# One explicit order for the first 2256 steps of a fused attention and MLP kernel

## The chip, the core and the metric

The kernel runs on one core of a Trainium2 chip. The core has a matrix engine (TensorE, called PE in the profile, with its weight loads as PEld), a vector engine (DVE), a scalar engine (ACT), GpSimd (POOL) and a queue that issues transfers (SP). Each engine works through its own list of instructions in the order in which the program issued them, and they wait for one another by semaphores. The metric is device time in microseconds (us) of the whole program; the median of three runs of the kernel before is 1229.67 us (1228.19 to 1231.2).

## The reference

Attention over 8 batches, 12 heads, 448 positions and 64 dimensions, with a root-mean-square norm on q and k, and then an MLP with ELU on the 3584 tokens of 768 features:

```python
q_n, k_n = rmsnorm(q, g_q), rmsnorm(k, g_k)
scores = matmul(q_n, k_n.transpose(0, 1, 3, 2)) / sqrt(64)
attn = softmax(scores)                       # minus the row's maximum, sum + 1e-9
x = matmul(attn, v).transpose(0, 2, 1, 3).reshape(3584, 768)
h = x @ w_in                                 # 768 x 2048
g = where(h > 0, h, exp(min(h, 0)) - 1)
out = g @ w_out                              # 2048 x 768
```

## The kernel before

Heads go in pairs: 48 pairs, six to a batch, and a pair has seven score tiles of 128 x 448, so there are 336 tiles T. Large products are made of float16 parts: a value is split into a high and a low half, and a product is three matmuls (high x high, high x low, low x high).

The steps, by the names that the text uses (lines are those of the profile):

- Per pair p: load q and k (L345), square them on ACT (`qk_square`, L368), sum (DVE, L372), root by logarithm and exponential on ACT (L376, L377), norm on POOL (L397), copies to float16 on ACT (L406, L416), low halves on POOL, transposes by transfer (L435), swapped halves (L442).
- Per tile T: the score matmuls (`s_mm`, L578), the row maximum on DVE (`s_max`, L585), the exponential on ACT (`s_exp`, L601), reciprocal (L613). The 42 tiles of batch 0 then make a scaled diagonal on POOL (`s_diag`, L617), are transposed by PE (`s_pe`, L625) and copied out by ACT (`s_hi`, L635). Later tiles are scaled by ACT (`s_hi`, L645), get a low half from DVE (`s_lo`, L651) and are transposed by transfers (`s_tr`, L661).
- Per pair: `attend` (L678) multiplies with v into the bank `av`; ACT and DVE write the result as x(p) in two halves (`x_high` L685, `x_low` L692 or L697).
- Weights: the 16 blocks of w_in and the 24 blocks of w_out are turned into high and low halves once, in the kernel's first part, each by nine steps (`conv`): a load (L244), two steps on ACT (L252, L255), steps on DVE (L260, L284), column sums on PE (L157), a scale on DVE, a high half on POOL (L300, L322) and a low half on DVE (L305, L327).
- MLP of a batch: the first layer has 16 blocks f, each of 18 matmuls (6 chunks of x by 3 parts, L778), and ELU on ACT and DVE (`m1_out`, L710 to L735). It takes x(0) to x(5) in turn, so no block is complete before x(5) is there. The second layer has 6 blocks of 48 matmuls (L789). A batch is 576 MLP matmuls, 4608 in all. MLP accumulators rotate over three banks (m0, m1, s4).

The order of issue is written by hand in a table, `SCHED`. A tile needs two half slots h, a pair 14, a batch 84. In the kernel before every step has a half slot (or a point half a slot ahead of one) in `tasks`; the loop runs over h from -18 and issues, for each h, the steps of h - 0.5, loads, the other steps, some MLP matmuls with the score matmuls and `attend` of that h in between them, and last the steps that use PE otherwise (`late`). Within a slot the order is that in which the steps were entered into `tasks`. How many MLP matmuls are issued up to a slot comes from a list (`rate`) until the list ends, then from `RATE` (576 per 84 half slots). Rows of the table that run out are repeated with their period.

Of the kernel before, what the change touches and what calls it, by code (L numbers as in the profile page):

```python
# [28 lines left out]
VSC = 6  # L29
# [4 lines left out]
def tile_attention_then_elu_mlp(ctx: ExitStack, tc: tile.TileContext, qk, v, v_scan, gg, w_in, w_out, out):  # L34
# [666 lines left out]
    def m1_out(b, f, ph):  # L701
# [37 lines left out]
        return SCHED["m1"][f if b == 0 else NF], [one, two, three, four, five]  # L739

    def m2_out(b, d, py):
# [19 lines left out]
        return SCHED["m2"][d if b == 0 else NC_], [one, two, three]  # L761
# [48 lines left out]
    def put(hs, steps):  # L810
        for h, (fn, *args) in zip(hs, steps, strict=True):
            at(h, fn, *args)

    at(-18, gains)
    for T in reversed(range(NCHUNK)):
        rows = SCHED["tile"]
        hs = rows[T] if T < len(rows) - 1 else [2 * T + h for h in rows[-1]]
        j = T % NJ
        if in_burst(T // NJ) and j < BURST:
            hs = [h + 1 - 0.5 * j for h in hs]  # L820
        if not by_pe(T):
            put(hs[:6], [(fn, T) for fn in (s_max, s_exp, s_z, s_rec, s_hi, s_lo)])


            at(hs[6] if len(hs) == 7 or 0 < j < NJ - 1 else hs[7 if j == 0 else 8], s_tr, T)
        else:
            put(hs[:7], [(fn, T) for fn in (s_max, s_exp, s_z, s_rec, s_diag, s_pe, s_hi)])
    for p in range(NP):
        k = p if p < 12 else 11
        put([h + HP * (p - k) for h in SCHED["qk"][k]], [  # L830
            (load_qk, p), (qk_square, p), (qk_sum, p), (qk_root, p), (qk_newton, p), (qk_norm, p),
            (k_high, p), (q_gain, p), (q_high, p), (k_low, p), (q_low, p), (qk_transpose, p, 0),
            (qk_transpose, p, 1), (q_swap, p),
        ])
        hs = [h + HP * (p - k) for h in SCHED["v"][k]]
        if not by_pe(p * NJ):
            put(hs[:5], [(load_v, p), (v_mult, p), (v_high, p), (v_low, p), (v_shift, p)])
        put(hs[5:], [(x_high, p), (x_low, p)])
    for b in range(B):
        k = min(b, 2)  # L840
        hs = [h + HB * (b - k) for h in SCHED["scan"][k]]
        put(hs[:VSC], [(scan_load, b, i) for i in range(VSC)])
        put(hs[VSC : 2 * VSC], [(scan_max, b, i) for i in range(VSC)])
        put(hs[2 * VSC :], [(fn,) for fn in v_steps(b)])
# [4 lines left out]
    for b in range(B):  # L849
        k = min(b, 1)  # L850
        hs = [h + HB * (b - k) for h in SCHED["m"][k]]
        put(hs, [(fn,) for fn in m_steps(b)])
# [5 lines left out]
    moe = mlps()  # L858

    def due(h):  # L860

        n = SCHED["rate"][0]
        i = h - RATE_FROM
        if i < 0:
            return 0
        return n[i] if i < len(n) else int((h - START) * RATE)

    pe_at = {}
    for T in range(NCHUNK):
        n = SCHED["mm"][0]  # L870
        if in_burst(T // NJ) and T % NJ < BURST:
            if T % NJ == 0:
                pe_at.setdefault(2 * T, []).append((s_burst, T // NJ))
            continue
        pe_at.setdefault(n[T] if T < len(n) else 2 * T - 1, []).append((s_mm, T))
    for p in range(NP):
        n = SCHED["att"][0]
        pe_at.setdefault(n[p] if p < len(n) else HP * p + HP + 7, []).append((attend, p))

    START = HB + X_LAG  # L880
    H0, LAST = -18, 2 * NCHUNK + 28
    done = 0
    ctx.enter_context(tc.manual_schedule())
    for h in range(H0, LAST):
# [4 lines left out]
        want = due(h + 1)  # L889
# [15 lines left out]
    for r in moe:  # L905
        done += 1
        if r:
            put([h + x for x in r[0]], [(fn,) for fn in r[1]])
# [3 lines left out]
    for h in range(h + 1, h + 9):  # L912
# [4 lines left out]
SCHED = {  # L917
# [15 lines left out]
        [0, 22, 20, 30.5, 47.5, 24.5, 32],  # L933
        [-2.5, 32.5, 34, 23, 27.5, 38, 41],
        [11, 20.5, 25.5, 5.5, 26, 55, 57],
        [61, 63, 78.5, 57.5, 74, 72, 72.5],
        [68.5, 83, 58, 63, 58, 78.5, 80.5],
        [56, 58, 74, 69, 75, 90.5, 91.5],
        [67, 94, 96.5, 97, 97, 107.5, 107.5],
        [94, 109, 110.5, 113.5, 113.5, 122, 124],  # L940
        [109, 120, 126, 126, 129.5, 137.5, 140],
        [135.5, 127, 134, 146.5, 138.5, 148.5, 154],
        [106, 139, 141.5, 146, 154.5, 165.5, 171],
# [248 lines left out]
```

## Time and profile before

| what | value |
|---|---|
| median of three runs | 1229.67 us |
| the profiled execution | 1230.09 us |
| its span, first to last instruction | 1228.2 us |
| PE busy | 1177.8 us (96%) |
| DVE busy | 920.7 us (75%) |
| ACT busy | 811.0 us (66%) |
| POOL busy | 522.6 us (43%) |
| granted TensorE clock, mean of the run | 0.996 |

Busy is the time in which at least one instruction of the engine was under way; instructions of one engine overlap a little, so the durations of a group sum to more than its busy time. The span less PE's busy time is 50.4 us: the time in which PE had nothing under way. A view by stretches shows where that is and what the others do meanwhile; the chain of waits says what the end was waiting for at each time. A granted clock of 1.00 is 2.4 GHz, and PE has only that level and half of it; a number between is a mean over a stretch.

### The profile page before, as it was taken

Reading aid. Unit: us, or ns where it says so; the run is one execution under the profiler, and the core shown is the slowest. Engines: PE = TensorE matmul, PEld = TensorE weight load, DVE = VectorE, ACT = ScalarE, POOL = GpSimd, SP = SyncE. Lnnn points to the kernel's source line nnn. Section 1 sums busy time; section 2 is a strip of 40 time slices with the busy share of each in tenths; the row PEclk is TensorE's granted clock in tenths of the full one; section 3 lists DMA queues with packets and bytes.
Section 4 is the critical chain, followed back from the end, with each engine's and each line's share of the span. In section 5 each row is a group of like instructions: output and inputs, shape, how many; then the busy total and the mean of one; then the engine's idle time right before and its main releaser. Section 6 shows DMA issues by size and latency. Waiting matters only on the chain.

```text
span 1228.2 us, 21622 instructions
## 1 busy us (share of the span) xinstructions
PE 1177.8 (96%) x7180; PEld 720.9 (59%) x7180; DVE 920.7 (75%) x2042; ACT 811.0 (66%) x1705; POOL 522.6 (43%) x789
## 2 busy tenths in 40 slices
PE   2888899999999999999999999999999999999998
PEld 1655455775457645665557645665557645675576
DVE  7999999877996699767996699767996699642510
ACT  7999999767775477556775477556775477542310
POOL 4676655644444354444444354444444354320000
PEclk9899999999999999999999999999999999999999
DMA  9766887889668877687768867787668866560000
GB/s 304 226 196 164 209 176 166 187 171 186 135 135 169 187 138 137 144 198 149 139 128 169 188 139 136 141 200 151 138 128 169 189 139 139 112 111 26 1 16 30
DMA packets 405744, 183.24 MB, mean 149 GB/s; under 512 B 368896, under 2 KB 388096, under 8 KB 405632
## 3 DMA queue, kind: packets, MB, share of 16 engines
q1 hardware_dynamic: 405632, 181.86, 67.6%
q8 instruction: 57, 0.93, 0.3%
q14 instruction: 55, 0.45, 0.1%
HBM read 68.35 MB, written 11.01 MB: 65 GB/s over the span
## 4 chain that ended last, share of the span: by engine, by line
PE 81%; DVE 5%; issue 1%; ACT 0%; DMA 0%; SPq 0%; POOL 0%; ACTq 0%
PE m L789 23%; PE m L778 21%; PE s L789 12%; PE s L778 10%; PE av L678 7%; PE s L578 4%; PE s L562 2%; PE s L567 1%; DVE p L651 1%; DVE st L585 1%; DVE gall L735 1%; DVE w32s L284 0%; DVE wlos L327 0%; DVE e L722 0%; DVE ss L372 0%
## 5 line engine op out<-in xcount | busy, mean ns | idle before, releaser
L789 PE MATMUL m<-gall,whos 128*128 128x448 f16 x1024 | 278.2, 353 | 0.0
L585 DVE TENSOR_REDUCE st<-s 128x1 f32<-128x448 f32 x336 | 205.9, 616 | 88.2 <-PE s L578 77.7
L605 POOL TENSOR_SCALAR st<-st 128x1 f32<-128x1 f32 x294 | 77.1, 262 | 456.5 <-ACT w32s L601 389.9
L789 PEld LDWEIGHTS <-whos 128*128 128x128 f16 x1536 | 222.0, 145 | 69.7 <-issue 0.7
L778 PE MATMUL m<-x,whi 128*128 128x448 f16 x926 | 252.8, 352 | 0.3 <-DVE e L722 0.3
L778 PEld LDWEIGHTS <-whi 128*128 128x128 f16 x1536 | 149.7, 98 | 135.6 <-issue 1.7
L601 ACT ACTIVATE w32s<-s,st 128x448 f32<-128x448 f32 x242 | 152.2, 629 | 72.7 <-DVE st L585 71.9
L651 DVE SCALAR_TENSOR_TENSOR raws<-w32s,st,raws 128x448 f16<-128x448 f32 x199 | 170.6, 857 | 37.4 <-ACT raws L645 36.6
L789 PE MATMUL m<-gall,wlos 128*128 128x448 f16 x512 | 182.0, 355 | 0.0
L778 PE MATMUL m<-x,wli 128*128 128x448 f16 x463 | 163.4, 353 | 0.0
L645 ACT ACTIVATE raws<-w32s,st 128x448 f16<-128x448 f32 x199 | 130.8, 661 | 12.9 <-ACT raws L645 6.9
L789 PE MATMUL s<-gall,whos 128*128 128x448 f16 x512 | 139.0, 353 | 0.0
L789 PEld LDWEIGHTS <-wlos 128*128 128x128 f16 x768 | 110.6, 144 | 47.1 <-issue 13.1
L578 PE MATMUL s<-qkt 128*64 128x448 f16 (+1 forms) x496 | 111.2, 365 | 14.3 <-ACT gall L635 5.5
L778 PE MATMUL s<-x,whi 128*128 128x448 f16 x450 | 122.4, 352 | 0.0
L778 PEld LDWEIGHTS <-wli 128*128 128x128 f16 x768 | 75.0, 98 | 79.0 <-issue 13.1
L732 ACT ACTIVATE gall<-e,ui 128x448 f16<-128x448 f32 x128 | 85.2, 665 | 52.0 <-DVE e L727 52.0
L735 DVE SCALAR_TENSOR_TENSOR gall<-e,ui,gall 128x448 f16<-128x448 f32 x128 | 89.7, 701 | 9.3 <-ACT gall L732 8.3
L678 PE MATMUL av<-ptall,vt 128*64 128x448 f16 x924 | 95.3, 353 | 1.3 <-DVE most L160 0.6
L397 POOL TENSOR_TENSOR nat<-nat,r 128x896 f32<-128x896 f32 (+1 forms) x48 | 84.4, 1759 | 22.0 <-DVE r L387 13.6
L789 PE MATMUL s<-gall,wlos 128*128 128x448 f16 x256 | 90.9, 355 | 0.0
L710 ACT ACTIVATE e<-m,sc 128x448 f32<-128x448 f32 x86 | 53.9, 627 | 49.0 <-PE m L778 49.0
(133 smaller groups left out, 1957.9 us busy)
## 6 DMA issues: line engine op xcount, KB each, us to landing
nat<-in_qk SPq DMA_DIRECT2D x48, 448.0 KB, 4.7
raws<-in_w_out SPq DMA_DIRECT2D x24, 512.0 KB, 4.2
qkt<-qkt SPq DMA_DIRECT2D x96, 112.0 KB, 4.3
out<-y SPq DMA_DIRECT2D x48, 224.0 KB, 2.4
vn<-in_v SPq DMA_DIRECT2D x38, 256.0 KB, 2.9
vscan<-in_v_scan SPq DMA_DIRECT2D x36, 224.0 KB, 3.3
whos<-in_w_in SPq DMA_DIRECT2D x10, 768.0 KB, 7.0
raws<-in_w_in SPq DMA_DIRECT2D x6, 768.0 KB, 7.8
```

Source lines behind the costliest of these rows:

```text
L397: nc.gpsimd.tensor_tensor(out=n[:, a:], in0=n[:, a:], in1=r[:, a:], op=ALU.mult)
L578: nc.tensor.matmul(ps[r0 : r0 + n, :S], lhs, qq[:, 1, h * S : h * S + S], start=(t == 0), stop=(t == 2),)
L585: nc.vector.tensor_reduce(out=st[:, 0:1], in_=pss[T][:, :S], axis=AX.X, op=ALU.max, negate=True)
L601: nc.scalar.activation(e, ps, AF.Exp, bias=st[:, 0:1], accum_out=st[:, 1:2])
L605: (nc.vector if by_pe(T) else nc.gpsimd).tensor_scalar(out=st[:, 1:2], in0=st[:, 1:2], scalar1=1e-9, scalar2=2.0 ** (UP - 7) if by_pe(T) e ...
L645: nc.scalar.activation(p16[:, :S], e, AF.Copy, scale=stats[T][:, 2:3])
L651: nc.vector.scalar_tensor_tensor(out=p16[:, S:], in0=e, scalar=r, in1=p16[:, :S], op0=ALU.mult, op1=ALU.subtract)
L678: nc.tensor.matmul(av[64 * h : 64 * h + 64, :S], vs[:, h], ps[h], start=(k == 0), stop=(k == len(terms) - 1),)
L732: nc.scalar.activation(g[:, 0], e, AF.Copy, scale=ui)
L735: nc.vector.scalar_tensor_tensor(out=g[:, 1], in0=e, scalar=ui, in1=g[:, 0], op0=ALU.mult, op1=ALU.subtract)
L778: nc.tensor.matmul(ph[:, :S], w[:, c, :], x[:, r, :], start=(c == 0 and i == 0), stop=last)
L789: nc.tensor.matmul(py[:, :S], w, g[:, r, :], start=(f == 0 and i == 0), stop=last)
```

## The change

The first 2256 steps are now issued one by one: each has a number from -2256 to -1 in the table, and the numbers are issued in turn. The score matmuls of a tile, an `attend` and each triple of MLP matmuls have numbers too. From half slot 240 the loop is the same as before. Half slots under 240, with the list `rate`, are gone. The numbered part holds 338 triples, 1014 MLP matmuls, as many as the loop before had issued when it came to slot 240, and from `x_low` of pair 16 on both programs have issued the same work. Steps are neither added nor taken out.

```diff
-        return SCHED["m1"][f if b == 0 else NF], [one, two, three, four, five]
+        return "m1", b * NF + f, [one, two, three, four, five]
...
-        return SCHED["m2"][d if b == 0 else NC_], [one, two, three]
+        return "m2", b * NC_ + d, [one, two, three]
...
-    tasks = {}
-
-    def at(h, fn, *args):
-        tasks.setdefault(h, []).append((fn, args))
-
+    first, tasks, pe_at = {}, {}, {}
     loads |= {load_qk, load_v, scan_load}
+    def at(x, fn, *args):
+        if x < 0:
+            first[x] = fn, args
+        else:
+            tasks.setdefault(x, []).append((fn, args))
...
+    def pe(x, fn, i):
+        if x < 0:
+            first[x] = fn, (i,)
+        else:
+            pe_at.setdefault(x, []).append((fn, i))
+
+    def row(name, i, pitch, own):
+        rows = SCHED[name]
+        if i < len(rows) - 1:
+            return rows[i]
+        return [x + pitch * (i - own) for x in rows[-1]]
...
-    def due(h):
-
-        n = SCHED["rate"][0]
-        i = h - RATE_FROM
-        if i < 0:
-            return 0
-        return n[i] if i < len(n) else int((h - START) * RATE)
-
-    pe_at = {}
+    done = 0
+
+    def mlp_step(h=0):
+
+        nonlocal done
+        r = next(moe, None)
+        done += 1
+        if r:
+            name, i, fns = r
+            rows = SCHED[name]
+            put(rows[i] if i < len(rows) - 1 else [h + x for x in rows[-1]], [(fn,) for fn in fns])
+
+    def mlp_three():
+        for _ in range(3):
+            mlp_step()
+
+    for x in SCHED["mlp"]:
+        at(x, mlp_three)
...
-        pe_at.setdefault(n[T] if T < len(n) else 2 * T - 1, []).append((s_mm, T))
+        n = SCHED["mm"]
+        pe(n[T] if T < len(n) else 2 * T - 1, s_mm, T)
...
+    for x in range(-FIRST, 0):
+        fn, args = first.pop(x)
+        fn(*args)
     for h in range(H0, LAST):
...
-        want = due(h + 1)
+        want = int((h + 1 - START) * RATE)
...
-                r = next(moe, None)
-                done += 1
-                if r:
-                    put([h + x for x in r[0]], [(fn,) for fn in r[1]])
+                mlp_step(h)
...
-        [0, 1, 3, 4.5, 4.5, 6.5, 8],
+        [-2199, -2188, -2187, -2186, -2179, -2178, -2163],
...
+    "mlp": [
+        -1915, -1831, -1737, -1693, -1549, -1527, -1526, -1523, -1519, -1518, -1517, -1516,
...
+FIRST, H0 = 2256, 240
```

What moves is best seen where x(5), the last chunk that the first layer of batch 0 needs, is written. In the kernel before, ACT's list has these rows up to the step that writes it (`x5`, L685) and one behind. The names: `s0` to `s4` are the score banks, `p16` a scaled tile of batch 1, `raws` and `wts` a block of w_out under conversion, `st` a tile's statistics, `ln` and `r0` the root of a later pair's norm, `dg` a diagonal for the scale of v, `gall` the transposed tiles of batch 0. It is the 191st step on ACT's list.

```order
L635 ACTIVATE gall_131<-s1_68 112x4x128
L645 ACTIVATE p16_1626<-s2_69,st_1555 128x448
L376 ACTIVATE ln_1628<-ss_1614,eps_85 128x14
L377 ACTIVATE r0_1629<-ln_1628 128x14
L601 ACTIVATE s3_70,st_1582<-s3_70,st_1582 128x448
L484 ACTIVATE dg_1638<-ident_75,m1_1602 128x128
L252 ACTIVATE wts_134<-raws_133 128x512
L601 ACTIVATE s4_71,st_1651<-s4_71,st_1651 128x448
L255 ACTIVATE raws_133<-raws_133 128x512
L645 ACTIVATE p16_1674<-s3_70,st_1582 128x448
L685 ACTIVATE x5_128<-av_72,vs_474 128x448
L252 ACTIVATE wts_134<-raws_133 128x512
```

In the changed kernel the same place of ACT's list reads as follows; `x5` is the 178th step.

```order
L635 ACTIVATE gall_131<-s1_68 112x4x128
L255 ACTIVATE raws_133<-raws_133 128x512
L601 ACTIVATE s2_69,st_1512<-s2_69,st_1512 128x448
L255 ACTIVATE raws_133<-raws_133 128x512
L252 ACTIVATE wts_134<-raws_133 128x512
L685 ACTIVATE x5_128<-av_72,vs_700 128x448
L484 ACTIVATE dg_1621<-ident_75,m1_1357 128x128
L601 ACTIVATE s3_70,st_1539<-s3_70,st_1539 128x448
L645 ACTIVATE p16_1630<-s2_69,st_1512 128x448
L601 ACTIVATE s4_71,st_1573<-s4_71,st_1573 128x448
L252 ACTIVATE wts_134<-raws_133 128x512
L645 ACTIVATE p16_1658<-s3_70,st_1539 128x448
```

Between the last copy of batch 0 (`gall`) and `x5` nine steps stood; now four do, and the scaled tiles of batch 1, the diagonal and two exponentials have gone behind `x5`.

On PE the second place is the first layer of batch 0, just behind its first block. In the kernel before the list reads so (`m1` is the accumulator of block 1, `x3` and `x4` chunks of x, `whi1` and `wli1` the block's weights, `s2` a score bank, `qkt` a pair's transposed q and k):

```order
L778 MATMUL m1_74<-x2_125,wli1_106 128x448
L778 LDWEIGHTS whi1_90
L778 MATMUL m1_74<-x3_126,whi1_90 128x448
L578 LDWEIGHTS qkt_1560
L578 MATMUL s2_69<-qkt_1560 128x448
L578 LDWEIGHTS qkt_1560
L578 MATMUL s2_69<-qkt_1560 128x448
L778 LDWEIGHTS whi1_90
L778 MATMUL m1_74<-x3_126,whi1_90 128x448
L778 LDWEIGHTS wli1_106
L778 MATMUL m1_74<-x3_126,wli1_106 128x448
```

In the changed kernel the same MLP matmuls stand together:

```order
L778 MATMUL m1_74<-x2_125,wli1_106 128x448
L778 LDWEIGHTS whi1_90
L778 MATMUL m1_74<-x3_126,whi1_90 128x448
L778 LDWEIGHTS whi1_90
L778 MATMUL m1_74<-x3_126,whi1_90 128x448
L778 LDWEIGHTS wli1_106
L778 MATMUL m1_74<-x3_126,wli1_106 128x448
L778 LDWEIGHTS whi1_90
L778 MATMUL m1_74<-x4_127,whi1_90 128x448
```

A score pair that stood between two parts of one triple is gone from there. From `x5` to the first matmul of the second layer PE had 44 score matmuls, 66 of `attend` (three pairs) and 102 of column sums between the MLP matmuls, and now has 35, 44 and 84.

## Rows read from the trace of the kernel before

**Rows 1.** The page: busy time of each engine over the whole span

```profile
PE 1177.8 (96%) x7180; PEld 720.9 (59%) x7180; DVE 920.7 (75%) x2042; ACT 811.0 (66%) x1705; POOL 522.6 (43%) x789
```

**Rows 2.** View by stretches: first and last us, length, then busy us (instructions)

```profile
core 0: us, PE busy (x) PEld busy (x) DVE busy (x) ACT busy (x) POOL busy (x), PEclk, DMA share, GB/s
0.00:20.00 20.00, 2.14 (x27) 1.59 (x27) 13.10 (x35) 13.74 (x17) 5.76 (x10) 1.00 0.81 268
20.00:40.00 20.00, 12.61 (x88) 8.30 (x89) 19.22 (x47) 18.65 (x34) 16.03 (x17) 0.83 1.02 327
40.00:60.00 20.00, 17.65 (x147) 13.26 (x146) 17.92 (x49) 18.13 (x35) 12.23 (x15) 0.91 0.68 214
60.00:143.00 83.00, 68.12 (x587) 45.50 (x587) 77.53 (x219) 81.87 (x159) 58.46 (x66) 1.00 0.67 183
143.00:200.00 57.00, 53.50 (x371) 29.14 (x370) 55.03 (x131) 54.84 (x107) 30.16 (x43) 1.00 0.87 191
200.00:240.00 40.00, 40.00 (x261) 26.03 (x260) 36.10 (x85) 35.76 (x71) 21.40 (x33) 1.00 0.75 162
```

**Rows 3.** Chain of waits, 0 to 240 us: start, length, what

```profile
195.09 1.11 DVE gall L735
196.20 0.61 DVE e L722
196.85 0.92 PE m L778 x4
```

**Rows 4.** ACT in order of time where x(5) is written: start, duration, instruction

```profile
138.93 1.36 ACT L255 ACTIVATE raws<-raws 128x512 uint16<-128x512 uint16 x1
140.02 0.65 ACT L645 ACTIVATE p<-s,st 128x448 f16<-128x448 f32 x1
140.55 0.64 ACT L685 ACTIVATE x<-av,vs 128x448 f16<-128x448 f32 x1
141.07 0.68 ACT L252 ACTIVATE wts<-raws 128x512 f32<-128x512 f32 x1
```

**Rows 5.** DVE there, in order of time

```profile
141.68 0.67 DVE L692 SCALAR_TENSOR_TENSOR x<-av,vs,x 128x448 f16<-128x448 f32 x1
```

**Rows 6.** PE there, in order of time

```profile
142.19 0.56 PE L778 MATMUL m<-x,whi 128*128 128x448 f16 x2
```

**Rows 7.** ACT by line, 0 to 143 us: count, busy, mean ns, idle before

```profile
L601 ACT ACTIVATE ex<-s,st 128x448 f32<-128x448 f32 x42 | 26.8, 639 | 0.9 <-DVE st L585 0.4 <-PE s L625 0.4
...
L255 ACT ACTIVATE raws<-raws 128x512 uint16<-128x512 uint16 x10 | 13.5, 1354 | 0.0
L635 ACT ACTIVATE ptall<-s 112x512 f32<-112x512 f32 x21 | 13.0, 623 | 1.8 <-PE s L625 1.8
...
L601 ACT ACTIVATION_READ_ACCUMULATOR ex<-s,st 128x1 f32 x42 | 8.7, 208 | 0.0
L252 ACT ACTIVATE wts<-raws 128x512 f32<-128x512 f32 x10 | 6.8, 684 | 0.1
L368 ACT ACTIVATE qkt<-nat 128x896 f32<-128x896 f32 x7 | 6.7, 961 | 1.0 <-PE s L578 1.0
...
L406 ACT ACTIVATE t<-nat 128x448 f16<-128x448 f32 x8 | 4.8, 598 | 0.0
L416 ACT ACTIVATE t<-nat 128x448 f16<-128x448 f32 x8 | 4.6, 573 | 0.0
...
L376 ACT ACTIVATE ln<-ss,eps 128x14 f32<-128x14 f32 x9 | 2.7, 305 | 0.1
...
L377 ACT ACTIVATE r<-ln 128x14 f32<-128x14 f32 x9 | 1.9, 215 | 0.3
L645 ACT ACTIVATE p<-s,st 128x448 f16<-128x448 f32 x3 | 1.9, 638 | 0.0
```

**Rows 8.** The page: DVE line 651 with both inputs in SBUF, mean ns after the busy us

```profile
L651 DVE SCALAR_TENSOR_TENSOR raws<-w32s,st,raws 128x448 f16<-128x448 f32 x199 | 170.6, 857 | 37.4 <-ACT raws L645 36.6
```

**Rows 9.** DVE line 651 with one input in PSUM: least, median, greatest ns

```profile
L651 DVE SCALAR_TENSOR_TENSOR p<-s,st,p x52: 658/675/686, 137.3 to 310.3; 128x448 f16<-128x448 f32 x52
```

More of the change, by code (lines that the diff above doesn't have):

```diff
@@ L808, in run_tasks @@
                 fn(*args)
[L810 to L814, printed above, removed]
+    at(SCHED["gains"], gains)
     for T in reversed(range(NCHUNK)):
-        rows = SCHED["tile"]
-        hs = rows[T] if T < len(rows) - 1 else [2 * T + h for h in rows[-1]]
         j = T % NJ
[L819 to L825, printed above, removed]
-        else:
-            put(hs[:7], [(fn, T) for fn in (s_max, s_exp, s_z, s_rec, s_diag, s_pe, s_hi)])
+        xs_ = row("tile", T, 2, 0)
+        if T >= len(SCHED["tile"]) - 1:
+            if in_burst(T // NJ) and j < BURST:
+                xs_ = [x + 1 - 0.5 * j for x in xs_]
+            xs_ = xs_[:6] + [xs_[6] if 0 < j < NJ - 1 else xs_[7 if j == 0 else 8]]
+        if by_pe(T):
+            fns = s_max, s_exp, s_z, s_rec, s_diag, s_pe, s_hi
+        else:
+            fns = s_max, s_exp, s_z, s_rec, s_hi, s_lo, s_tr
+        put(xs_, [(fn, T) for fn in fns])
     for p in range(NP):
-        k = p if p < 12 else 11
-        put([h + HP * (p - k) for h in SCHED["qk"][k]], [
+        put(row("qk", p, HP, 11), [
             (load_qk, p), (qk_square, p), (qk_sum, p), (qk_root, p), (qk_newton, p), (qk_norm, p),
@@ L834, in tile_attention_then_elu_mlp @@
         ])
-        hs = [h + HP * (p - k) for h in SCHED["v"][k]]
+        xs_ = row("v", p, HP, 11)
         if not by_pe(p * NJ):
-            put(hs[:5], [(load_v, p), (v_mult, p), (v_high, p), (v_low, p), (v_shift, p)])
-        put(hs[5:], [(x_high, p), (x_low, p)])
+            put(xs_[:5], [(load_v, p), (v_mult, p), (v_high, p), (v_low, p), (v_shift, p)])
+        put(xs_[-2:], [(x_high, p), (x_low, p)])
     for b in range(B):
[L840 to L844, printed above, removed]
+        xs_ = row("scan", b, HB, 2)
+        put(xs_[:VSC], [(scan_load, b, i) for i in range(VSC)])
+        put(xs_[VSC : 2 * VSC], [(scan_max, b, i) for i in range(VSC)])
+        put(xs_[2 * VSC :], [(fn,) for fn in v_steps(b)])
     for f in range(NF):
@@ L849, in tile_attention_then_elu_mlp @@
     for b in range(B):
-        k = min(b, 1)
-        hs = [h + HB * (b - k) for h in SCHED["m"][k]]
-        put(hs, [(fn,) for fn in m_steps(b)])
+        put(row("m", b, HB, 1), [(fn,) for fn in m_steps(b)])
     def mlps():
@@ L904, in tile_attention_then_elu_mlp @@
     h = LAST - 1
[L905 to L908, printed above, removed]
+    while done < MLP_STEPS:
+        mlp_step(h)
         if done % 7 == 0:
@@ L932 @@
     "v": [
[L933 to L943, printed above, removed]
+        [-1985, -1945],
+        [-1883, -1869],
+        [-1799, -1768],
+        [-1698, -1696],
+        [-1614, -1595],
+        [-1551, -1537],
+        [-1459, -1458, -1426, -1322, -1335, -1267, -1203],
+        [-1250, -1249, -1248, -1168, -1139, -1025, -1004],
+        [-1338, -1337, -1247, -1064, -1241, -876, -866],
+        [-1068, -1067, -915, -892, -848, -798, -758],
+        [-1238, -1237, -850, -825, -819, -679, -631],
+        [-794, -750, -749, -728, -739, -589, -587],
+        [-655, -538, -537, -535, -516, -396, -323],
+        [-532, -471, -470, -406, -367, -256, -175],
+        [-324, -237, -235, -186, -184, -99, -84],
+        [-157, -156, -121, -118, -100, -22, -10],
+        [-117, -89, -88, -86, -79, 246.5, 247.5],
+        [-46, 247.5, 248.5, 249.5, 251, 260.5, 261.5],
         [152.5, 163.5, 164.5, 165.5, 167, 176.5, 177.5],
@@ new lines @@
+        [-327, -282, -281, -227, -226, -221, -182],
+        [-274, -273, -225, -214, -212, -200, -137],
+        [-270, -269, -248, -247, -205, -191, -147],
+        [-231, -223, -174, -173, -171, -161, -98],
+        [-222, -195, -112, -111, -110, -109, -77],
+        [-211, -208, -207, -192, -168, -140, -123],
+        [-210, -189, -172, -164, -134, -116, -101],
+        [-199, -158, -105, -85, -75, -74, -73],
+        [-150, -149, -131, -83, -72, -51, -32],
+        [-113, -108, -107, -106, -44, -41, -30],
@@ L1128 @@
     "m2": [
-        [6, 8.5, 8.5],
-        [11, 13.5, 18.5],
-        [2, 11, 15.5],
-        [7, 9.5, 15.5],
-        [3, 4, 13],
-        [2.5, 6.5, 11],
+        [-1023, -1022, -887],
+        [-878, -852, -851],
+        [-879, -752, -712],
+        [-696, -695, -581],
+        [-673, -621, -602],
+        [-616, -595, -573],
+        [-136, -135, -103],
+        [-53, -52, -37],
+        [-4, 240, 241],
         [1, 2, 3],
@@ L1137 @@
     "mm": [
[5 rows of a table removed]
[10 rows of a table added]
+    ],
+    "burst": [
+        -414, -279, -153, -15,
     ],
     "att": [
-        [20, 35, 50, 62, 76, 90, 104, 118, 131, 147, 162, 175],
+        -1987, -1900, -1846, -1724, -1640, -1564, -1276, -1121, -974, -826, -702, -596, -458,
+        -277, -148, -33,
+    ],
+    "mlp": [
[25 rows of a table added]
     ],
```

289 lines of the change are left out of this document (166 added, 123 removed), and 171 rows, old and new, of the table SCHED.

## The prediction

> **What bounds the kernel now.** I read the page's totals first, then the view by stretches, then the chain of waits, then the rows around one place. The totals say that PE is busy 1177.8 of 1228.2 us [rows 1], so 50.4 us of the span are left that an order of issue could win, no more. The reader is to see in the stretches [rows 2] where they lie. To 143 us PE is busy 2.14 + 12.61 + 17.65 + 68.12 = 100.5 us, idle 42.5. From 143 to 200 it is idle 57 - 53.5 = 3.5 us, from 200 to 240 not at all, and 50.4 - 42.5 - 3.5 = 4.4 us are left for the remaining thousand. Behind 200 us PE alone sets the time. Ahead of it ACT does: it is idle 60 - 50.5 = 9.5 us in the first 60 us, and then 83 - 81.87 = 1.1 us to 143 us. DVE is close behind with 127.8 us of work to 143 us against ACT's 132.4. The chain says the same: it runs through DVE and ACT until 196.85 us and through PE from there [rows 3].
>
> What ends PE's idle time is x(5), since no block of the first layer is complete without it. ACT writes its high half at 140.55 us [rows 4], DVE its low half at 141.68 [rows 5], and the dense MLP matmuls begin at 142.19 [rows 6]. ACT came to that step without a pause from 60 us on, so the time of x(5) is the amount of ACT work that stands ahead of it, with the 9.5 us of the start.
>
> **The change part by part.** No step is added or taken out, and the amount of work of each engine is the same. So the question is what stands ahead of x(5), what stands between x(5) and PE's full stretch, and what new pauses the order makes.
>
> *Ahead of x(5).* On ACT's list the step that writes x(5) was the 191st and is now the 178th. The 13 that went behind it are two `s_bits` of w_out (L255), one `s_act` (L252), two exponentials with their sums (L601), two scaled tiles of batch 1 (L645), one square of q and k (L368), one logarithm and one exponential of a norm (L376, L377), two copies to float16 (L406, L416) and a diagonal that I leave at nothing. With the means of [rows 7]: 2 x 1.354 + 0.684 + 2 x (0.639 + 0.208) + 2 x 0.638 + 0.961 + 0.305 + 0.215 + 0.598 + 0.573 = 9.0 us. These are durations, and ACT starts the next step before the last has ended: L255 took 1.36 us and the next began after 140.02 - 138.93 = 1.09, L645 took 0.65 and the next began after 0.53 [rows 4], so 0.81 of a duration counts. That makes 7.3 us, with 9.0 as the other end. DVE's list shrinks ahead of its half of x(5) as well, from 342 steps to 325, so it does not stay behind as the later of the two. First term: 7.3 us off.
>
> *From x(5) to the second layer.* ACT's list has 125 steps there and now 110, DVE's 174 and 155, beside the same MLP matmuls of PE: five exponentials and five scaled tiles fewer on ACT, nine score matmuls and one `attend` fewer on PE. In this stretch PE waited 3.5 us in all [rows 2]. I take all of it as gone (other end: nothing gone). Second term: 3.5 us off.
>
> *The first 60 us.* The 9.5 us of ACT's idle time at the start are waits for the first loads and for the chain from q and k to the first tiles, and I leave them as they are. PE's own order there costs nothing: PE was busy 32.4 of 60 us, under ACT's work. That its granted clock was a mean of 0.83 from 20 to 40 us and 0.91 from 40 to 60, where it paused between short groups, and 1.00 behind [rows 2], is covered in the same way. The cover is gone when ACT has to wait for PE, which is the next point.
>
> *New pauses.* A tile of batch 0 leaves ACT (exponential), passes DVE, POOL and PE and comes back to ACT (copy, L635); if ACT has too little else to do meanwhile, it waits, and everything behind it on its list waits too. Summing ACT's steps between the two along either list with the durations of [rows 7] less the overlap, the middle tile of the 42 had 6.7 us of other work and now has 5.4, and four tiles instead of two have 3.0 or less. The row for the first batch of these copies shows 1.8 us of waits for PE over 21 tiles [rows 7]. Ends: nothing, if the shorter distances still suffice, and 3.6 us, twice that row. I take half of that row, 0.9 us, since of the short distances in the trace some had a wait and some had none. Third term: 0.9 us on.
>
> *Transfers.* SP's list moves with the steps. Ahead of the load of pair 2's q and k there stand five weight blocks of 768 KB instead of four and two pieces of v of 256 KB: 256 KB more, which at the 327 GB/s of 20 to 40 us [rows 2] is 0.8 us. ACT's list has 16 steps between the squares of pair 1 and of pair 2 to cover it, so I count nothing, and 0.8 us if they don't.
>
> *Behind slot 240* nothing moves, and PE had no idle time there that could swallow the gain, so it reaches the end.
>
> Sum: 7.3 + 3.5 - 0.9 = 9.9 us off the profiled execution, 1230.09 - 9.9 = 1220.2. The median of the runs shown lies 0.4 us under that execution: 1219.8 us.
>
> **The rivals.**
>
> *DVE and POOL hinder each other more.* A low half that reads two tiles from SBUF takes 857 ns in the mean [rows 8], while the same line with one input in PSUM takes 675 and never more than 686 [rows 9]; the work is equal, so the 0.18 us come from company. Ahead of x(5) DVE has 43 such steps (16 low halves and 16 joins of w_in, 7 joins and 4 low halves of w_out). If the new order puts POOL's steps beside them as often as the late tiles have it, DVE has 43 x 0.18 = 7.7 us more. DVE's work to x(5) is then 127.8 - 6.4 (17 of 342 steps at the mean) + 7.7 = 129.1 us and ACT's 132.4 - 7.3 = 125.1: DVE is last, and the first term falls to 132.4 - 129.1 = 3.3. Time: 1219.8 + 4.0 = 1223.8. For it speaks that POOL is the engine whose place in the order nobody sees on PE; against it, that those steps show little of it so far in the stretch where POOL is busy 58 of 83 us.
> The Trainium skill, "SBUF — State Buffer", section "Who interferes with whom", has the rule behind this: a DVE instruction with two SBUF inputs contends with a GpSimd instruction that reads SBUF, and whoever comes first keeps the port for its whole instruction. The two means above agree with that; by the rule the loss could be a whole POOL instruction at a time.
>
> *The pauses take it all.* From 60 to 143 us ACT is busy 99% and DVE 93%, and an order fixed step by step lets every delay of one pass to the others. If ACT waits the 0.9 us taken above not once but at every fourth of the 42 tiles, that is 9.5 us, and the time is 1219.8 - 0.9 + 9.5 = 1228.4, no change. For it: the shorter distances. Against: ACT ran 83 us with 1.1 us idle under an order that was no looser in kind.
>
> *Transfers make it slower.* If ACT runs dry in the first 60 us because each of the five weight blocks ahead of pair 2's q and k must pass first (768 KB at 327 GB/s is 2.4 us, five are 12 us) and one more does so ahead of pair 3, 14.4 us are lost against 9.9 won: 1219.8 + 14.4 = 1234.2. It decides from 12.4 us more idle time of ACT in that stretch. For it: transfers were under way on all engines from 20 to 40 us (share 1.02 [rows 2]). Against: pair 3 has the same seven weight blocks ahead of it as before and four pieces of v fewer, and in the kernel before ACT lost 3.2 us from 20 to 60 us.
>
> *More than forecast.* If the start also loses 3 of its 9.5 idle us and the full durations count, 9.0 + 3.5 + 3 = 15.5 us: 1214.2.
>
> **How the numbers follow.** Forecast 0.66, DVE and POOL 0.14, more than forecast 0.06, no change 0.07, slower 0.07. A difference under 0.2%, 2.5 us, cannot be told from none here. Faster: 0.66 + 0.14 + 0.06 = 0.86; same 0.07; slower 0.07. The forecast's own range, from the ends of its terms, is 1217.2 (9.0 + 3.5) to 1226.8 (7.3 - 3.6 - 0.8). To hold 8 in 10 I go from 1213.5, beyond the greater gain, to 1227, past the rival with DVE and short of no change.
>
> **What would show it.** Right: in the profile after, the step that writes x(5) is reached near 133 us instead of 140.6, PE's idle time to there is some 35 us instead of 42.5, and PE stays without a gap from there on; the chain of waits turns to PE at x(5), not at 197 us. First term wrong: ACT idle between 60 us and x(5) beyond 2 us, or x(5) later than 137. Second term wrong: PE idle over 2 us in the 57 us behind x(5). DVE rival: the mean of L305, L284 or L327 up by more than a tenth, and the low half of x(5) over 2 us behind the high half. Transfers: ACT waiting for `nat` or `raws` more than in the first 10 us. The prediction is wrong if the time is above 1227, or if it is right with x(5) no earlier than before.

## The result and the profile after

| kernel | median | executions | ratio to before, 95% interval |
|---|---|---|---|
| before | 1229.94 us | 1228.19 to 1231.2 | 1 |
| changed | 1248.67 us | 1245.73 to 1250.11 | 1.0150 [1.0126, 1.0174] |

The changed kernel is 18.7 us slower; 1219.8 was forecast. The profiled execution took 1250.11 us (before: 1230.09). The page of the changed kernel, busy time of each engine, against [rows 1]:

```profile
PE 1188.6 (95%) x7180; PEld 728.0 (58%) x7180; DVE 925.3 (74%) x2042; ACT 814.4 (65%) x1705; POOL 514.0 (41%) x789
```

The work is the same, and PE's idle time rose from 50.4 to 1248.3 - 1188.6 = 59.7 us. Its busy time rose by 10.8 us as well: 6.4 of them lie ahead of the dense MLP matmuls (106.1 us instead of 99.7), where PE ran at its lower clock for part of the time (see below). The view by stretches of the changed kernel, against [rows 2]:

```profile
core 0: us, PE busy (x) PEld busy (x) DVE busy (x) ACT busy (x) POOL busy (x), PEclk, DMA share, GB/s
0.00:20.00 20.00, 1.71 (x26) 1.58 (x27) 11.43 (x33) 12.46 (x16) 4.69 (x9) 1.00 0.68 230
20.00:40.00 20.00, 14.99 (x99) 10.72 (x99) 15.70 (x43) 15.57 (x29) 12.90 (x14) 0.83 0.88 244
40.00:60.00 20.00, 13.32 (x111) 9.49 (x109) 17.30 (x47) 18.52 (x38) 14.73 (x17) 1.00 0.88 261
60.00:143.00 83.00, 69.81 (x549) 47.09 (x550) 72.14 (x186) 72.62 (x134) 42.57 (x55) 0.92 0.63 162
143.00:200.00 57.00, 53.80 (x359) 29.01 (x358) 52.28 (x127) 52.68 (x102) 28.65 (x41) 1.00 0.68 163
200.00:240.00 40.00, 37.90 (x254) 24.83 (x252) 35.53 (x82) 33.81 (x66) 16.62 (x25) 1.00 0.84 161
240.00:300.00 60.00, 56.20 (x356) 39.02 (x356) 51.97 (x124) 45.05 (x95) 34.03 (x56) 0.97 1.02 208
300.00:420.00 120.00, 116.17 (x672) 67.15 (x670) 94.19 (x202) 80.47 (x178) 49.79 (x80) 1.00 0.75 145
```

The same view of the kernel before, of the two stretches that were not shown:

```profile
240.00:300.00 60.00, 59.44 (x366) 39.34 (x365) 48.75 (x110) 37.80 (x85) 29.45 (x48) 1.00 0.88 187
300.00:420.00 120.00, 119.67 (x695) 72.14 (x693) 95.26 (x206) 78.75 (x177) 49.97 (x83) 1.00 0.76 153
```

Two things stand out. From 60 to 143 us ACT is busy 72.62 instead of 81.87 us: it no longer runs without a pause. And from 200 to 420 us, where PE was idle 0.9 us before (0 + 0.56 + 0.33), it is now idle 2.1 + 3.8 + 3.8 = 9.7 us.

Where x(5) is written (line by line in order of time; answers to [rows 5, 6]), DVE and then PE:

```profile
149.55 0.68 DVE L692 SCALAR_TENSOR_TENSOR x<-av,vs,x 128x448 f16<-128x448 f32 x1
150.28 0.35 PE L778 MATMUL m<-x,whi 128*128 128x448 f16 x1 [0.18 <-DVE x L692]
```

DVE's half came at 141.68 us before: it is 7.9 us later, not 6.4 earlier.

For the comparisons below I read four points from each profiled execution: A, the start of the 16th matmul of L778, where the dense MLP matmuls begin; B, the first matmul of layer 2 (L789); C, the 285th of L789, near the end of batch 0's layer 2; D, the 570th, about slot 240. From D to the end of the span every kernel takes the same 805 us.

| kernel | median us | A | B | C | D | A to C | C to D |
|---|---|---|---|---|---|---|---|
| before | 1229.94 | 142.2 | 215.5 | 283.5 | 422.9 | 141.3 | 139.4 |
| changed | 1248.67 | 149.8 | 216.8 | 299.2 | 443.0 | 149.4 | 143.8 |

So 7.6 us are lost ahead of A, 8.1 from A to C and 4.4 from C to D: 20.1 in all. B alone misleads. Counting PE's matmuls at the pitch of a dense stretch (189 ns for one of 448 columns), PE has some 68 us of work from A to B before and some 63 in the changed kernel: about 5 us were put behind B, and the 1.3 us of lag at B hide that backlog. From A to D the work is equal (271.6 and 272.0 us), and the time above it is 9.1 us before and 21.2 after.

Part of the 7.6 us ahead of A comes and goes with PE's clock. From 60 us to A, the changed kernel and `late_scores` (below; its order is the same up to x(5)):

```profile
60.00:149.80 89.80, 76.12 (x609) 51.38 (x610) 78.77 (x206) 79.25 (x146) 44.43 (x59) 0.92 0.62 161
60.00:145.70 85.70, 69.72 (x606) 46.73 (x606) 78.89 (x205) 77.93 (x144) 44.91 (x57) 1.00 0.62 168
```

DVE and ACT are busy for nearly the same time in both, PE for 6.4 us more in the first. There its granted clock was 0.5, the lower level (1.2 GHz), from 73.9 to 77.3, from 90.9 to 94.3 and from 121.6 to 128.5 us, 13.7 us in all; ahead of each of these falls PE had been idle for 2.2 to 2.8 of 5 us. In the three executions that kept 1.00 from 60 us on with the changed kernel's steps of each engine ahead of x(5) (`late_scores`, `less_dve_after`, and `less_loads_after`, which leaves loads out), A came at 145.7, 146.4 and 146.8 us, 3.5 to 4.6 us later than before; with 13.7 us at the lower level it came at 149.8 (`a_to_layer2`: 148.4). So about half of the 7.6 us is there at the full clock. Whether the lower clock made the other waits longer or followed from them is not shown.

### The profile page after: what moved, and what is told of

Its sections match the earlier page's. It is cut to its first block, busy times and chain, and to the rows that moved or that the text cites. A ratio compares the mean times of both kernels' runs of the same rounds, so it can differ in the third digit from the quotient of the medians.

```text
span 1248.3 us, 21612 instructions
## 1 busy us (share of the span) xinstructions
PE 1188.6 (95%) x7180; PEld 728.0 (58%) x7180; DVE 925.3 (74%) x2042; ACT 814.4 (65%) x1705; POOL 514.0 (41%) x789
## 4 chain that ended last, share of the span: by engine, by line
PE 66%; DMA 0%; DVE 0%; ACT 0%; issue 0%; ACTq 0%
PE m L789 19%; PE m L778 18%; PE s L789 9%; PE s L778 9%; PE av L678 5%; PE s L578 3%; PE s L562 2%; PE s L567 1%; DMA ptall<-raws 0%; DVE raws L651 0%; ACT y L756 0%; ACT raws L645 0%; DVE st L585 0%; PE av L157 0%; ACT w32s L601 0%
## 5 line engine op out<-in xcount | busy, mean ns | idle before, releaser
L789 PE MATMUL m<-gall,whos 128*128 128x448 f16 x1024 | 277.5, 353 | 0.0
L789 PEld LDWEIGHTS <-whos 128*128 128x128 f16 x1536 | 221.0, 145 | 70.8 <-issue 2.2
L778 PE MATMUL m<-x,whi 128*128 128x448 f16 x926 | 251.5, 353 | 2.3 <-DVE x L692 0.9
L778 PEld LDWEIGHTS <-whi 128*128 128x128 f16 x1536 | 149.0, 98 | 137.1 <-issue 3.5
L651 DVE SCALAR_TENSOR_TENSOR raws<-w32s,st,raws 128x448 f16<-128x448 f32 x199 | 171.6, 862 | 39.2 <-ACT raws L645 38.4
L789 PE MATMUL m<-gall,wlos 128*128 128x448 f16 x512 | 181.7, 355 | 0.0
L778 PE MATMUL m<-x,wli 128*128 128x448 f16 x463 | 163.6, 353 | 0.0
L789 PE MATMUL s<-gall,whos 128*128 128x448 f16 x512 | 138.9, 353 | 0.0
L789 PEld LDWEIGHTS <-wlos 128*128 128x128 f16 x768 | 110.5, 144 | 45.9 <-issue 11.7
L778 PE MATMUL s<-x,whi 128*128 128x448 f16 x450 | 121.9, 352 | 0.0
L778 PEld LDWEIGHTS <-wli 128*128 128x128 f16 x768 | 75.1, 98 | 79.8 <-issue 12.5
L397 POOL TENSOR_TENSOR nat<-nat,r 128x896 f32<-128x896 f32 (+1 forms) x48 | 81.8, 1704 | 23.5 <-DVE r L387 17.8
L789 PE MATMUL s<-gall,wlos 128*128 128x448 f16 x256 | 90.8, 355 | 0.0
```

The lines of the kernel that those rows point to most:

```text
L397: nc.gpsimd.tensor_tensor(out=n[:, a:], in0=n[:, a:], in1=r[:, a:], op=ALU.mult)
L651: nc.vector.scalar_tensor_tensor(out=p16[:, S:], in0=e, scalar=r, in1=p16[:, :S], op0=ALU.mult, op1=ALU.subtract)
L778: nc.tensor.matmul(ph[:, :S], w[:, c, :], x[:, r, :], start=(c == 0 and i == 0), stop=last)
L789: nc.tensor.matmul(py[:, :S], w, g[:, r, :], start=(f == 0 and i == 0), stop=last)
```

## The experiments

Eighteen kernels ran. Where only the order changes, each step keeps a place of its own in a list, and the diff is told in words.

**Which stretch of the order costs what: b_to_x5, a_to_x5, b_to_layer2, a_to_layer2.** Each takes one kernel's order up to a step, and then the rest of the steps in the other's.

```diff
-one order for the first 2256 steps
+b_to_x5, a_to_x5: before's (changed) order through x_low(5), the rest in the changed (before's) one
+b_to_layer2, a_to_layer2: the same, up to the first matmul of layer 2
```

> The steps up to x(5) in the order of the kernel before, all others in the order of the changed kernel (338 triples still end at slot 240, nothing left out). In the changed kernel x(5) came 7.9 us late and the rest of the numbered part lost 12.2 us more. Theory 1 (the numbered order makes engines wait for each other all along, each part for itself): the first loss goes, the second stays, 1249 - 8 = 1241 us, ACT idle to x(5) near 11 us. Rival (the first part's lateness causes the later waits, since later steps are planned against it): both go, about 1230 us.

> The steps up to the first matmul of the second layer (288 MLP matmuls) in the changed order, all others in the order of before. At that matmul the changed kernel was 1.3 us later than before, with one attend and five tiles less done, which makes PE's backlog 6.8 us greater. Theory 1: only that backlog is lost, 1230 + 7 = 1237 us, and PE idle from there to slot 240 under 2 us. Rival (the late start goes on costing): 1249 us, PE idle there still near 10 us.

> The counterpart: the order of before up to the first matmul of the second layer, the changed order from there to slot 240. Theory 1: loses what the changed kernel lost behind that matmul, 20.1 - 6.8 = 13 us, 1243 us, with PE waiting for score banks (low halves L651) and transposes as in the changed kernel. Rival (the later part is as good as before if it starts on time): 1230 us.

> The changed order through the low half of x(5), before's behind it: the missing corner beside b_to_x5 (1240.6). If the two parts' losses add, 1230 + 8 = 1238. If the steps that the changed order puts behind x(5) meet before's score matmuls, as in defer_only (7.7 us), 1245 or more.

| kernel | median us | ratio | A | B | C | D | A to C | C to D |
|---|---|---|---|---|---|---|---|---|
| b_to_x5 | 1240.61 | 1.0089 [1.0074, 1.0104] | 142.4 | 206.6 | 289.2 | 432.1 | 146.8 | 142.9 |
| a_to_x5 | 1246.59 | 1.0128 [1.0112, 1.0143] | 159.9 | 232.8 | 300.8 | 439.6 | 140.9 | 138.8 |
| b_to_layer2 | 1237.81 | 1.0068 [1.0054, 1.0083] | 143.8 | 217.0 | 288.1 | 432.2 | 144.3 | 144.1 |
| a_to_layer2 | 1254.78 | 1.0205 [1.0191, 1.0218] | 148.4 | 215.5 | 309.1 | 447.8 | 160.7 | 138.7 |

b_to_x5 splits the loss: 10.7 us behind x(5), the other 8.1 ahead of it. C to D takes 142.9 to 144.1 us wherever the changed order stands there, and 138.7 or 138.8 where before's does: these 4 to 5 us are local. The two that begin with the changed order and go on with before's paid at the seam: the put-off steps crowd in behind it. PE's waits in a_to_x5, from 149 to 233 us (columns: us in total, times, longest):

```profile
PE s L578 <- DVE p L651: 11.4, 2, 10.5
```

A score matmul stood in PE's list, ahead of dense MLP matmuls, and its bank was freed by a scaled tile (L651) that had been put off. So these two say nothing of the loss in the changed kernel, and my 1237 for a_to_layer2 missed for that reason in part. In a_to_layer2 PE's granted clock was also 0.50 from 220.4 to 240.9 us, where PE was busy for 10.1 us; the two causes were not separated.

**The first term by itself: defer_only.**

```diff
+before's order; the 37 steps that the changed order puts behind x(5) stand right behind x_low(5)
```

> The order of before, with one thing taken from the changed order: the 37 steps that stand ahead of x(5) before and behind it in the changed kernel are put right behind x(5). This is the first term of the forecast alone. If it was right as a mechanism and only the new waits hid it: x(5) 5 to 7 us earlier than 142.4, and 1223 to 1227 us. Rival (what is put off comes back ahead of the second layer, on the same engines): x(5) earlier, but 1229 to 1231 us. Rival (the displaced steps had covered waits): x(5) no earlier than 140, 1230 us or more.

1237.61 us, 1.0066 [1.0052, 1.0080]: slower. DVE's half of x(5) ended 3.0 us sooner (139.4 us), but A came at 148.0, 5.8 later. PE's waits from 139 to 222 us:

```profile
PE s L578 <- DVE p L651: 11.1, 3, 8.5
```

It is the same stop. Less work ahead of x(5) starts the dense matmuls sooner only if no score matmul in PE's list ahead of them needs a bank from the steps put off.

**Ahead of x(5): start_b, far_copies, early_scores, less_dve_in_after.** ACT's waits in the changed kernel, 0 to 60 us (to the second line of dots) and then 60 to 150.3 us:

```profile
ACT wts L252 <- DMA raws<-in_w_in: 3.8, 1, 3.8
ACT ptall L368 <- DMA nat<-in_qk: 2.3, 1, 2.3
ACT ptall L635 <- PE s L625: 1.8, 2, 0.9
...
ACT gall L635 <- PE s L625: 0.9, 1, 0.9
...
ACT ptall L635 <- PE s L625: 2.4, 1, 2.4
ACT ex L601 <- DVE st L585: 2.2, 2, 1.5
ACT ex L601 <- PE s L625: 2.0, 2, 1.5
ACT qkt L368 <- DMA nat<-in_qk: 1.7, 1, 1.7
...
ACT gall L635 <- PE s L625: 0.5, 2, 0.3
```

The same view of the kernel before, 60 to 142.4 us:

```profile
ACT ex L601 <- PE s L625: 0.4, 1, 0.4
ACT wts L252 <- DMA raws<-in_w_in: 0.2, 1, 0.2
ACT ex L601 <- DVE st L585: 0.2, 1, 0.2
```

In all ACT is idle 24.0 us to x(5), against 10.6 before. The four kernels ask which of these pauses is the cause.

```diff
+start_b: before's order through x_low(0), then the changed one
+far_copies: 29 of the 42 copies (L635) later on ACT's list
+early_scores: 24 score matmuls of batch 0 directly behind the copy that frees their bank
```
```diff
         def s_low(w, ws):
+            if f >= 2:
+                return
...
-                for i, (w, r) in enumerate(((wh, 0), (wh, 1), (wl, 0))):
+                for i, (w, r) in enumerate(((wh, 0), (wh, 1), (wh, 0))):
```

> Before's order through the low half of x(0), then the changed order. Theory 1a (the loss ahead of x(5) is made in the start, where x(0) came at 73.9 us instead of 65.0): x(5) is back near 142 to 144 us and the time near 1241. Rival 1b (it is made tile by tile by short distances between exponential and copy, 10.6 us of idle ACT behind 60 us): x(5) at 147 to 150, time 1245 to 1249.

> Changed order, but 29 of the 42 copies (L635) of batch 0's tiles are moved back on ACT's list until 6.5 us of other ACT work stand between a tile's exponential and its copy where the neighbours allow (the middle tile goes from 4.6 to 6.4 us, before had 5.9 by the same count). Theory 1b (ACT's waits for PE at the copies, 7.7 us ahead of x(5), come from the short distance): they fall to 2 or 3, x(5) near 145, time near 1244. Rival 1a (they come from the tile's own chain being late from the start, so the wait moves to the next step): no change, 1248 to 1250.

> The changed order, but 24 of the score matmuls of tiles 5 to 41 (batch 0) come directly behind the copy that frees their bank, as far as q and k of the pair are there. Theory 3 (the five score banks are the bound ahead of x(5): each is held 10 us from maximum to copy and then stands empty until the next maximum, 140 us summed over 37 refills against 115 before, so 25/5 = 5 us of the 8 us): the empty time falls by 36 us or more to 105, the last copy comes 7 us sooner, time near 1242. Rival (the next maximum waits for DVE or for PE's other work anyhow, or PE now stops at the score matmul and holds up the other tiles): no change, 1247 to 1251.

> The changed kernel with 14 of the 16 low halves of w_in left out (L305, 1.007 us each, 14 us of DVE's work ahead of x(5); layer 1 uses the high half in their place, PE has the same matmuls). Theory 5 (ahead of x(5) the changed order is bound by no engine's work but by the engines' waits for each other): x(5) comes at most 4 us sooner, time 1244 to 1250. Rival (DVE's work sets x(5) there): 8 us or more sooner, time 1241 or less.

| kernel | median us | ratio | A | ACT idle to x(5) |
|---|---|---|---|---|
| start_b | 1244.97 (1240.27 to 1248.68) | 1.0115 [1.0080, 1.0149] | 148.6 | 23.3 |
| far_copies | 1258.43 | 1.0227 [1.0211, 1.0242] | 158.8 | 32.1 |
| early_scores | 1249.39 | 1.0157 [1.0139, 1.0174] | 150.0 | 24.3 |
| less_dve_in_after | 1248.38 | 1.0146 [1.0128, 1.0164] | 146.5 | 21.0 |

With before's start x(0) is back at 65.3 us (65.0 before, 73.9 in the changed kernel), and in the profiled execution x(5) is only 1.1 us sooner than in the changed kernel: most of ACT's idle time moved from the start to behind it. But the four executions of start_b are split: 1248.68 (the profiled one) and 1248.20 us, and 1241.75 and 1240.27, the time that was expected if the start is the cause and that b_to_x5 has. No trace of the second pair was kept. So the start is neither shown to be the cause nor cleared. Copies that come later do not end the waits, they lengthen them: a tile keeps its bank from its maximum to its copy, 9.8 us in the middle in the changed kernel and 11.9 in far_copies. Filling the freed banks sooner gave nothing, nor did 14 us less work for DVE. What pins x(5) in the changed order stays open. For the copies, the banks and DVE's work the experiments only exclude; start_b excludes nothing.

**Behind x(5), the places of the score matmuls: late_scores, late_scores_b.**

```diff
+31 groups of score matmuls behind x(5): up to three more triples of MLP matmuls ahead of them
```

> Changed order, but 31 of the groups of score matmuls behind x(5) are moved behind three more triples of MLP matmuls in PE's list (never past their own maximum). In the changed order the middle one of the score matmuls of tiles 47 to 97 stands directly behind the step that frees its bank, with no MLP matmul between, against six in the kernel before. Theory 1 (PE, in order, stops at a score matmul whose bank is not yet free): from the first matmul of layer 2 to slot 240, 8.2 us of PE's waits were for the scaled tiles (L651) and exponentials (L601) that free banks; most of it goes, time near 1241. Rival (the steps that free the banks are late wherever PE's matmuls stand, and the later score matmul only makes the next tile late): no change, 1248 to 1250, or slower.

> The order of b_to_x5 (before's through x(5), then the changed one), with the same move of the score matmuls. Theory 1: b_to_x5 reached layer 2 3.4 us ahead of the kernel before and lost 12 us of it behind, 9.7 us of it in waits for banks (L651 and L601); most of these go, time near 1233. Rival: unchanged near 1240.6 or slower. Under 1228 it would beat both kernels.

1249.06 us, 1.0152 [1.0137, 1.0167], and 1241.55, 1.0092 [1.0075, 1.0109]: no change against the changed kernel and b_to_x5. As far as a shift by three triples can tell, PE's stops at these matmuls are where the lateness shows, not where it is made.

**DVE's work behind x(5): less_dve_after, less_dve_before.**

```diff
         def s_low(w, ws):
+            if i >= 6:
+                return
...
-                for i, (w, r) in enumerate(((wh, 0), (wh, 1), (wlo[d][:, :, f], 0))):
+                for i, (w, r) in enumerate(((wh, 0), (wh, 1), (wh, 0))):
```

> The changed kernel with 18 of the 24 low halves of w_out (L327, 15 us of DVE's work, all of them behind x(5)) left out; layer 2 uses the high half in their place, so PE has the same matmuls. Theory 2 (behind x(5) DVE is as much a bound as PE until the attention output of batch 1 is complete, and the changed order has put 14 us of DVE's work behind the start of layer 2): PE's waits there fall from 17.5 us to 6 or less, the lag behind before at slot 240 from 20 to 9 us, time near 1238. Rival (the waits come from where PE's own matmuls stand, DVE has time): no change, 1247 to 1250.

> The kernel before with the same 18 low halves left out. Theory 2: PE waits 9.4 us between x(5) and slot 240, half of it for attend's pitch; 3 to 5 us go, time near 1226. Rival: no change, 1229 to 1231. The difference between this pair shows what DVE's time is worth in either order.

1247.39 us, 1.0131 [1.0108, 1.0155], not told apart from the changed kernel; and 1228.19, 0.9986 [0.9976, 0.9996], 1.7 us off the kernel before. Theory 2, by which DVE's work costs some 10 us behind x(5), falls. DVE's work is worth 1 or 2 us in either order.

**Behind x(5), the loads of w_out: less_loads_after, less_loads_before, less_both_after.** ACT's waits in the changed kernel, 150 to 300 us:

```profile
ACT wts L252 <- DMA raws<-in_w_out: 6.6, 5, 2.5
ACT p L645 <- DMA ptall<-p: 6.3, 7, 2.4
```

and in the kernel before, 142.4 to 284 us:

```profile
ACT p L645 <- DMA ptall<-p: 3.8, 4, 1.4
ACT wts L252 <- DMA raws<-in_w_out: 1.2, 1, 1.2
```

One such wait in the changed kernel, in order of time: SP issues the load, and ACT stands at its first step on that block until the load has landed.

```profile
251.54 0.81 SPq L244 DMA_DIRECT2D raws<-in_w_out  x2
...
256.24 0.69 ACT L252 ACTIVATE wts<-raws 128x512 f32<-128x512 f32 x1 [2.55 <-DMA raws<-in_w_out]
```

In the kernel before (blocks 17 and 18, and ACT's step on 17) 9 us of ACT's other steps lie between:

```profile
186.44 1.77 SPq L244 DMA_DIRECT2D raws<-in_w_out  x2
...
195.73 0.68 ACT L252 ACTIVATE wts<-raws 128x512 f32<-128x512 f32 x1
```

A load lands 4.4 us after its issue (median of 14 in that stretch; 4.2 before). By the lists, no step of ACT stands between a load and ACT's first step on the block in 8 of the 24 blocks of w_out in the changed order, and one of 0.6 us in a ninth (the expectation of early_loads miscounts them as 11); the least before is 0.7.

```diff
         def load():
+            if width == WO_W and i >= 6:
+                return
```

> The changed kernel without the loads of w_out's blocks 6 to 23 (18 of 24, 512 KB each; the conversion steps work on what stands in the rooms, so ACT, DVE, POOL and PE have the same work). Theory 4 (behind x(5) the changed order makes ACT wait for w_out's loads, 5.9 us from layer 2 to its end against 1.2 before, and everything behind ACT's list with it): 5 us or more off, time near 1243. Rival (ACT has time there, the waits are slack): no change, 1247 to 1250.

> The kernel before without the same 18 loads. Theory 4: 0 to 1 us off, 1229 to 1230. Rival: no change, the same.

less_both_after leaves out these loads and the low halves of less_dve_after.

> The changed kernel without the 18 loads and without the 18 low halves of w_out of less_dve_after. If w_out's conversion as a whole (loads and DVE) is what PE waits for behind x(5), the two add up to 8 to 12 us, time 1237 to 1241. If the loss is spread over all engines' waits for each other, 1243 to 1248.

| kernel | median us | ratio | A | B | C | D | A to C | C to D |
|---|---|---|---|---|---|---|---|---|
| less_loads_after | 1241.02 | 1.0091 [1.0076, 1.0106] | 146.8 | 212.2 | 289.3 | 433.5 | 142.5 | 144.2 |
| less_loads_before | 1229.58 | 0.9991 [0.9982, 1.0001] | 144.2 | 217.3 | 285.4 | 424.6 | 141.2 | 139.2 |
| less_both_after | 1242.31 | 1.0097 [1.0081, 1.0114] | 147.9 | 212.9 | 289.5 | 432.9 | 141.6 | 143.4 |

These 18 loads cost the changed order 7.7 us and the old one nothing that can be measured. A to C falls from 149.4 to 142.5 us: 6.9 of the 8.1 us lost there (in early_scores, whose order behind x(5) is the changed kernel's, A to C took 147.2, so by that execution it is 4.7). A came 3.0 us sooner as well, at a granted clock of 1.00 from 60 us on, so a part of the 7.7 us may be the clock's. DVE's relief adds nothing to it. A load that is left out also takes its bytes and its place on SP's list away, so this does not show that ACT's wait is what costs.

**Moving the loads alone: early_loads, early_loads_b.**

```diff
+w_out's loads up on SP's list (22, and 17 in b), to 6 us of ACT's steps ahead of the first step on
+the block, or to 12 steps behind the join that frees the room
```

> The changed order with 22 of the 24 loads of w_out's blocks moved up on SP's list, until 6 us of ACT's steps stand between a load's issue and ACT's first step on it, or up to 12 steps behind the one that frees its room. Nothing is left out. Theory 4 (ACT reaches w_out's first step before the load has landed, since the order leaves 0.0 us of ACT's work between them in 11 of 24 blocks; a load lands some 4 us after its issue): most of less_loads_after's gain comes back without leaving out a load, time 1241 to 1244. Rival (the loads' bytes or SP's issues themselves were what cost, or a load that is issued sooner now holds up SP's transposes): 1247 to 1252.

> Before's order through x(5), then the changed order (b_to_x5, 1240.6), with 17 loads of w_out moved up in the same way. Theory 4: another 4 to 7 us off, 1234 to 1237; what is left against the kernel before is the 4 to 5 us that every run with the changed order loses from layer 2's end to slot 240. Rival: 1240 or more. Under 1228 it would beat both kernels.

1254.70 us, 1.0200 [1.0184, 1.0216], and 1247.79, 1.0144 [1.0127, 1.0161]: slower by 6 to 7 us than without the move. ACT's waits in early_loads, 149.5 to 306 us, then SP's in the same stretch:

```profile
ACT p L645 <- DMA ptall<-p: 12.8, 7, 4.4
...
ACT wts L252 <- DMA raws<-in_w_out: 3.0, 3, 2.3
```
```profile
SPq L244 <- DVE w32s L284: 8.9, 2, 6.4
...
SPq L244 <- DVE ws L166: 5.6, 2, 3.8
```

In the changed kernel, 150 to 300 us, SP's two lines are

```profile
SPq L244 <- DVE ws L166: 3.9, 1, 3.9
...
SPq L244 <- DVE w32s L284: 2.9, 1, 2.9
```

One place in early_loads where both stand close together: SP, then ACT.

```profile
184.73 7.16 SPq L244 DMA_DIRECT2D raws<-in_w_out  x2
191.98 2.07 SPq L435 DMA_TRANSPOSE qkt<-t  x1
...
198.23 9.06 SPq L661 DMA_TRANSPOSE ptall<-p  x5
...
202.77 0.63 ACT L645 ACTIVATE p<-s,st 128x448 f16<-128x448 f32 x1 [4.37 <-DMA ptall<-p]
```

ACT's waits for loads fell from 6.6 to 3.0 us, and those for the transposes of scaled tiles (L661) rose from 6.3 to 12.8. SP issues in order: a load that stands ahead of its time waits at the head of SP's list until DVE has freed its room (14.5 us in all, 6.8 in the changed kernel), and the transposes behind it wait too, with the buffers of the scaled tiles that ACT needs next. So the rival holds: moving the loads alone buys no time here. That it would pay if the join that frees the room came sooner as well was not tried. The Trainium skill, "DMA: Bandwidth & Descriptors", section "Rules for kernel authors", advises to issue a DMA early and to wait on it late; by that rule early_loads should have won. The measurement goes against it here, as the issue itself had a wait in front of it and other transfers behind it.

No version that does all the work beat the kernel before.

## Why the prediction was wrong

*First term (7.3 us off).* The size was nearly right and the effect was not. ACT's busy time to x(5) fell from 142.4 - 10.6 = 131.8 to 150.2 - 24.0 = 126.2 us: 5.6. But x(5) came later, and the tell-tale named for it, ACT idle over 2 us between 60 us and x(5), fired with 10.5.

*Third term, "New pauses" (0.9 us on): the step that failed first.* It measured 13.4 us (24.0 - 10.6). I had priced one kind of wait, that of ACT for PE at the copies, by the one row that showed it. That kind alone rose from 1.8 to 5.6 us (the rows of L635 above), just beyond the term's other end of 3.6 us more; the rest are kinds that I had put at nothing, for loads and for maxima among them. The kernel before shows almost no pauses there, and a row of it shows that a wait was avoided, not what an order that does not avoid it pays. What follows from what among them stays open. PE's clock belongs here too: I wrote that its cover is gone when ACT has to wait for PE, and then gave it no price. At its lower level for 13.7 us between 60 us and A, it goes with 3 to 4 of the 7.6 us.

*Second term (3.5 us off).* By the count of PE's work, the time above it from A to B fell from about 5 to about 4 us: some 1 us. In b_to_x5 it fell to about 1.5 us (64.2 us for some 62.7 us of work). But "nine score matmuls and one `attend` fewer", which I named, was about 5 us of PE's work moved behind B, and is no gain where PE is full.

*"Behind 200 us PE alone sets the time", and "Transfers": the step that failed with it.* PE had no idle time there before, so I took its waits as settled by PE. They were settled by an order in which ACT, DVE and SP kept just ahead. In the changed one they do not: A to D takes 12 us more above PE's work. For the transfers I looked at the loads ahead of pair 2's q and k and nowhere else; 18 of w_out's 24 loads cost 7.7 us in the changed order and nothing in the old one (shown by leaving them out). The 4 to 5 us from C to D are shown to be local to the order there; which wait makes them was not tried.

*The rivals.* DVE and POOL: no. L305 went from 1049 to 1007 ns in the mean, L327 from 860 to 793, and the low half of x(5) began 1.9 us behind the high one (1.1 before), under the 2 us named. "The pauses take it all" was right that ACT's pauses eat the gain ahead of x(5), at 9.5 us instead of 13.4, but the kind it named, at the copies, is 3.8 of them. "Transfers make it slower" had the right sign and the right queue but the wrong place: it looked for them in the first 60 us, where ACT's idle time rose by 4.0 us. I gave these two 0.14 together.

## What to carry to other kernels

When an order is replaced, list for each load and each transpose what stands between its issue and the first step that needs it, and ahead of it on the issuing queue, in the new order, along the whole program; a load may be too late for its reader and too early for its queue at once. An engine that shows no idle time in a tuned kernel is not the only bound there: others at 90% and more (DVE and ACT were both at 97% from A to B) can take its place at the first delay. Price new waits in an untried fixed order from what the engines depend on, not from the waits that a tuned order still shows.

## What the runs showed of the hardware

A transpose holds SP's list for 1.25 us (median of 432; the least is 1.19), a load of w_out for 0.33 to 0.60 us, so the list is a resource of its own: by the durations of its issues, with the waits that lie inside them, SP is taken for 37 of 42 us from the 144th matmul of layer 2 to C in the changed kernel, and for 26 of 33 us before. PE's granted clock was 0.92 in the mean from 60 to 143 us, against 1.00 before [rows 2], and 0.97 from 240 to 300, against 1.00. Neither mean is one of its two levels: the lower held for 13.7 us in the first stretch and for 3.4 us from 241.1 in the second, after pauses of PE. One order of issue can meet either: with the changed order ahead of x(5), three executions had 1.00 from 60 us to A and two had 13.7 us at the lower level there, and A came 1.6 to 4.1 us later in the two. The runs of the changed kernel go the same way, 1247.53 and 1245.73 us at a mean granted clock of 0.995 and 0.996, 1250.11 and 1249.81 at 0.990 and 0.991.
